# Taking turns between VectorE's SBUF copies and GpSimd's operations in a two-headed attention kernel

## The chip, the cores and the metric

The kernel runs on one core of a Trainium2 chip. A core has five engines with a queue of instructions each: TensorE (PE in the profile, its weight loads PEld), VectorE (DVE), ScalarE (ACT), GpSimd (POOL) and SyncE (SP, which only issues transfers here). Each engine works through its queue in order, and queues wait for each other by semaphores. The metric is the time of one execution on the device in microseconds, the median of several runs.

## The reference

Two attention blocks on inputs of 2048 tokens by 512 features, 32 heads of 16 features; their outputs stand side by side.

```python
def _A_ref(x, wqkv, wo):            # linear attention
    q, k, v = ...                   # x @ wqkv, split into 32 heads of 16
    phi = lambda t: jnp.where(t > 0, t + 1, jnp.exp(t)) + 1e-6
    pq, pk = phi(q), phi(k)
    kv = jnp.einsum("bhsd,bhse->bhde", pk, v)
    z = jnp.einsum("bhsd->bhd", pk)
    num = jnp.einsum("bhqd,bhde->bhqe", pq, kv)
    den = jnp.einsum("bhqd,bhd->bhq", pq, z)[..., None] + 1e-6
    return merge_heads(num / den) @ wo

def _B_ref(x, wqkv, wo):            # softmax attention, all 2048 keys
    q, k, v = ...
    p = _softmax(jnp.einsum("bhqd,bhkd->bhqk", q, k) * Dh ** -0.5)
    return merge_heads(jnp.einsum("bhqk,bhkd->bhqd", p, v)) @ wo

return jnp.concatenate([a, b], axis=-1)
```

## The kernel before

**The softmax block (B)** is nearly all of the work. The 32 heads are taken in four groups of eight (`Gp`). A unit is one group, one stretch of 512 queries (`c`) and the even or odd heads (`e_`), so there are 32 units. A unit has 64 blocks: 16 key tiles for each of four heads. A block is a score matmul (keys `KM` against queries `QT`, 128 keys by 512 queries), an exponential, and value matmuls (`VV`) that add into the PSUM bank `pPV` with the sum of the weights in a 17th column. Blocks go one of two ways:

- *ACT's way.* PE puts three or two blocks into the PSUM tile `pS0` or `pS1`, and one ACT instruction (L894) writes their exponentials to `PT`. One value matmul follows per block.
- *The way of VectorE and GpSimd.* PE puts a block into one of the two banks of `pD`. VectorE evicts it with a multiply and an add into 16-bit integers whose bits, read as floats, are a coarse exponential (`DI`, L806, "eviction" below). When two blocks are there, GpSimd adds two integer constants (`SHC`) to both in one operation of 128x1024 integers (L830, "shift" below), which gives two further copies of the coarse exponential at other phases. Three value matmuls follow per block, each with its own scaled copy of `VV`.

The two scaled copies of `VV` are made by VectorE from the first one (L573: 128x544 bf16, SBUF to SBUF, two for each of 16 groups of tiles). When a unit is finished, VectorE transposes `pPV` into `OT` (L989) and takes reciprocals (L994), and GpSimd multiplies (L995).

**The linear block (A)** is spread over the whole time as small jobs that use the same banks of `pD`. Where it needs phi, ACT takes an exponential into `EA` (L584), VectorE clamps it in place (L585: 128x256 or 128x512 bf16, SBUF to SBUF), and VectorE adds the positive part from PSUM (L587), which sets the bank free or is followed by the copy `VNa` (L599) that does. B's projections of later groups and the output projections (L673) are jobs of the same kind, and so is a small test of the inputs' size (`GR`, `FLG`). The keys' projection is spread over `KM` by 96 small transfers on SP's queue.

"Copies" below are the 32 instructions of L573 and the 48 of L585.

**What sets the order.** When the program is built, a planner lists for each engine what is ready, with an assumed duration, and picks the earliest start; between starts within 0.03 us the smaller priority goes first. What it picks goes into that engine's queue, and `Sched.add` derives the semaphore waits from what each operation reads and writes. An operation that reads a key waits for the last that wrote it, and one that writes it waits for all that read it. A key needs no memory behind it. The planner's constants:

- `DNEXT`: with fewer blocks left in a unit, VectorE's blocks are taken from the next unit. `ALAG`: no VectorE block is taken when a job of A or B is later than this (us).
- `P1`, `SH`: assumed durations of an eviction and a shift, for one or two blocks.
- `DEFER`, `FLOW`: a score round for ACT has priority 0 when its deadline is nearer than `DEFER` us (or all wanted banks of `pD` are free), and else `FLOW`. `DPR` is the priority of a score block for VectorE alone; jobs on PE have 2 to 2.5; rounds of value matmuls have 4, or 1 when `PVURG` or more blocks wait for theirs.

Between starts PE's gaps are filled with matmuls that only keep it busy (L1123, L1132).

Of the kernel before, what the change touches and what calls it, by code (L numbers as in the profile page):

```python
# [231 lines left out]
def bass_concat_heads__linear_attn_block__softmax_full_mha__prompt_kernel(nc, A_x, A_wqkv, A_wo, B_x, B_wqkv, B_wo, out):  # L232
# [12 lines left out]
    SHIFTS = (343, 685)  # L245
    VSCALE = (203.0 / 256.0, 161.0 / 256.0)
    UB = NT * 4
    DNEXT = 8
    DEND = 20
    TEND = 720.0  # L250
    ALAG = 20.0
    DLEAD = 1.0
    DBL = 3.0
    TRACE = None
# [5 lines left out]
    sch = Sched()  # L260
    es = contextlib.ExitStack()
    with es:
# [15 lines left out]
        VV = sb("VV", [128, 2, 3, NT * VST], BF)  # L278
        PT = sb("PT", [128, NPT, 5 * 512], F16)
        DI = sb("DI", [128, NDG, 3, 1024], I16)  # L280
        ZW = sb("ZW", [128, 32], BF)
        SHC = sb("SHC", [128, 4], I16)
# [6 lines left out]
        EA = sb("EA", [128, 2, 512], BF)  # L289
        OT = sb("OT", [128, 2, 512], F32)  # L290
        XN = OT.bitcast(BF)[:, 1, :].rearrange("p (x n) -> p x n", n=512)
        ZR = sb("ZR", [128, 2, 16], F32)
# [29 lines left out]
        def f32v(bk, n=512):  # L322
            return bk[0][:, bk[2]:bk[2] + n]
# [52 lines left out]
        for e_ in range(2):  # L376
            sch.add("dve", lambda e, e_=e_: e.tensor_reduce(PAR[:, e_:e_ + 1], ZMk[:].rearrange("p (a e) -> p e a", e=2)[:, e_, :],
                                                           axis=AX.X, op=ALU.max),
                    reads=["ZMk"], writes=[("PAR", e_)])
# [14 lines left out]
        T = {"pe": 0.0, "act": 0.0, "dve": 0.0, "pool": 0.0}  # L394
        cands = {k_: [] for k_ in T}
        tok = {}
        seq = [0]

        def push(eng, ready, prio, dur, run):
            seq[0] += 1  # L400
            cands[eng].append((ready, prio, seq[0], dur, run))

        class Job:

# [10 lines left out]
            def stage_done(self, i, end, bk, bi):  # L415
                if i == self.rel and bi is not None:
                    jfree[bi] = end + LAT
                for st, tk in self.gives:
                    if st == i:
                        tok[tk] = end + LAT  # L420
                if i + 1 < len(self.stages):
                    eng, dur, fn = self.stages[i + 1]
                    lat = LAT if eng != self.stages[i][0] else 0.0
                    push(eng, end + lat, self.prio if eng == "pe" else (0 if i + 1 <= self.rel and self.bank else min(self.prio, 2)), dur,
                         lambda st_, en_, fn=fn: (fn(bk), self.stage_done(i + 1, en_, bk, bi)))

        def f_pe(fn, reads):
            return lambda bk: sch.add("pe", lambda e: fn(e, bk), reads=reads, writes=[bk[3]])
# [2 lines left out]
            return lambda bk: sch.add(lane, lambda e: fn(e, bk), reads=[bk[3]] + list(reads), writes=writes)  # L431

        def f_op(lane, fn, reads=(), writes=()):
            return lambda bk: sch.add(lane, fn, reads=reads, writes=writes)

        MM, TRB = 0.2155, 0.0555
        PH = 0.11
        QK = 0.22
        pmode = [None]
        P1, SH = (0.61, 1.12), (1.1, 1.92)  # L440
        SLK = 0.0
        FMARG = 0.06
        DEFER, FLOW, DPR, DDEL = 0.5, 2.05, 3, 0
        PVR, PVMIN, PVURG = 3, 4, 24
        jfree = [0.0] * 2 + [None] * 5

        def copy_to(lane, out_fn, in_fn):
# [110 lines left out]
        def v4_job(t4, Gp, **kw):  # L558
            r = Gp % 2

            def mm(e, bk, i):
                tl, cc = divmod(i, 4)
                t = 4 * t4 + tl
                return e.matmul(f32v(bk)[:, tl * 128:(tl + 1) * 128], lhsT=xTb[:, cc, t * 128:(t + 1) * 128],  # L564
                                rhs=Wb[:, cc, 1024 + Gp * 128:1024 + Gp * 128 + 128], start=(cc == 0), stop=(cc == 3))
            ts = range(4 * t4, 4 * t4 + 4)
            st = halves(mm, [("Wb", 2)] + [("xTb", t) for t in ts], n=16, parts=2, dur=0.0555)
            v = [VV[:, r, k_, 4 * t4 * VST:(4 * t4 + 4) * VST] for k_ in range(3)]
            st.append(("dve", 0.6, f_ev("dve", lambda e, bk: e.tensor_copy(  # L569
                v[0].rearrange("p (h c) -> p h c", c=17)[:, :, 0:16],  # L570
                f32v(bk).rearrange("p (h d) -> p h d", d=16)), [("VV1", r)], [("VV", r, 0, t4)])))
            for k_ in range(2):
                st.append(("dve", 0.21, f_op("dve", lambda e, k_=k_: e.tensor_scalar(v[k_ + 1], v[0], VSCALE[k_], None, op0=ALU.mult),  # L573
                                             [("VV", r, 0, t4), ("VV1", r)], [("VV", r, k_ + 1, t4)])))
            return Job(st, [("xTb", t) for t in ts] + ([("pvdone", Gp - 2)] if Gp >= 2 else []), [(4, ("V", Gp, t)) for t in ts], rel=2, **kw)


# [2 lines left out]
        def phi_stages(c0, n, out_ap, okeys):  # L580
            q = ectr[0] % 2
            ectr[0] += 1
            return [
                ("act", 0.051 + n * 0.000833, f_ev("act", lambda e, bk: e.activation(EA[:, q, 0:n], f32v(bk)[:, c0:c0 + n], ACTF.Exp), [], [("EA", q)])),  # L584
                ("dve", 0.067 + n * 0.00026, f_op("dve", lambda e: e.tensor_scalar(EA[:, q, 0:n], EA[:, q, 0:n], 1.0, 1e-6, op0=ALU.min, op1=ALU.add),  # L585
                                               [("EA", q)], [("EA", q)])),
                ("dve", 0.067 + n * 0.00105, f_ev("dve", lambda e, bk: e.scalar_tensor_tensor(out_ap, f32v(bk)[:, c0:c0 + n], 0.0, EA[:, q, 0:n],  # L587
                                                                                          op0=ALU.max, op1=ALU.add), [("EA", q)], okeys))]

# [170 lines left out]
        def d_pick(at, used):  # L760
# [5 lines left out]
            if (ajobs and at > ajobs[0].ready + ALAG) or (bjobs and at > bjobs[0].ready + ALAG and bjobs[0].start_time() is not None):  # L766
                return None
            if u < NU - 1 and left[u] < DNEXT:
                u += 1
# [52 lines left out]
        def shifts(buf):  # L822
            s_ = gst[buf]
            n = len(s_["items"])
            if not s_["closed"] or s_["p1"] < n:
                return

            def go(st_, en_):
                w = 256 * n
                sch.add("pool", lambda e: e.tensor_tensor(  # L830
                    DI32[:, buf, 1:3, 0:w], DI32[:, buf, 0, 0:w].unsqueeze(1).broadcast_to([128, 2, w]),
                    SHC32[:].unsqueeze(2).broadcast_to([128, 2, w]), op=ALU.add),
                    reads=[("DI", buf, 0, i) for i in range(n)] + ["SHC"], writes=[("DI", buf, k_, i) for k_ in (1, 2) for i in range(n)])
                for k_ in (1, 2):
                    for i in range(n):
                        done(buf, k_, i, en_)
            push("pool", s_["t"] + LAT, 1, SH[n - 1], go)
# [147 lines left out]
        def unit_done(u, t_):  # L985

            xb = (u // 2) % 2
            Gp, c, e_ = unit(u)
            sch.add("dve", lambda e: e.transpose(OT[:, 0, :], PVb[:, 0:512]), reads=[("PV", g) for g in range(4)], writes=[("OT", 0)])  # L989
            pvopen[0] = t_ + LAT  # L990
            o = OT[:, 0, :].rearrange("p (b r) -> p b r", r=32)
            xn = XN[:, xb, :].rearrange("p (b r) -> p b r", r=32)
            zr = ZR[:, 0, 0:16]
            st = [("dve", 0.25, f_op("dve", lambda e: e.reciprocal(zr, o[:, :, 16]), [("OT", 0)], [("ZR", 0)])),  # L994
                  ("pool", 0.65, f_op("pool", lambda e: e.tensor_tensor(xn[:, :, 16 * e_:16 * e_ + 16], o[:, :, 0:16],  # L995
                                                                      zr.unsqueeze(2).broadcast_to([128, 16, 16]), op=ALU.mult),
                                    [("OT", 0), ("ZR", 0)], [("XN", xb, e_)]))]
            if e_ == 1:
                k = 4 * Gp + c
                st.append(("dve", 0.65, f_op("dve", lambda e: e.transpose(ON[:, k, :], XN[:, xb, :]), [("XN", xb, 0), ("XN", xb, 1)], on_keys(k))))  # L1000
            urgent.append(Job(st, [("ot", u - 1)] if u else [], [(1, ("ot", u))] + ([(2, ("on", Gp, c))] if e_ == 1 else []),
                              bank=False, ready=t_ + LAT, prio=0.5))
            if Gp == NGP - 1 and e_ == 1:
                fin = u == NU - 1
                for tl in range(4):
                    ln = ("dve", "act")[tl % 2] if fin else "dve"
                    urgent2.append(omm_job("b", 4 * c + tl, 1 + tl, [("on", Gp, c)], [(1, ("st", c, tl))], lane=ln))
# [135 lines left out]
        while True:  # L1143
            opts = []
            for eng in T:
                best = None
                for c_ in cands[eng]:
                    st = max(T[eng], c_[0])
                    k_ = (round(st / 0.05), c_[1], c_[2])
                    if best is None or k_ < best[0]:  # L1150
                        best = (k_, st, c_)
                if best is not None:
                    c_ = best[2]
                    opts.append(pe_opt(best[1], c_[1], c_[3], c_[4], c_, "f") if eng == "pe" else (best[1], c_[1], eng, c_[3], c_[4], c_))
# [28 lines left out]
            st, _, eng, dur, run_, c_ = o  # L1183
            if c_ is not None:
                cands[eng].remove(c_)
            if eng == "pe":
                filler(st - T["pe"])
            T[eng] = st + dur
            run_(st, st + dur)
            npick += 1  # L1190
            if TRACE is not None:
# [88 lines left out]
```

## Time and profile before

| | |
|---|---|
| time, median of 3 runs | 759.22 us (758.39 to 762.62) |
| profiled execution: its own time | 765.03 us |
| profiled execution: span from first to last instruction | 763.3 us |
| mean granted PE clock in it | 0.97 |
| instructions profiled | 15604 |

All rows of the profile come from that one execution. "Busy" is the time in which an engine's instructions run, and an instruction that is held after its start counts as busy. "Idle before" of a group is the time for which its engine stood still just before its instructions, with the engine and line that ended it. PE's instructions overlap each other, so PE's busy share is no measure of how full it is.

### The profile page before, as it was taken

How to read it: one execution, taken by the hardware profiler on the slowest of the kernel's cores; microseconds unless marked ns; L12 is line 12 of the kernel's file. 1: busy time of each engine (PE TensorE's matmuls, PEld its weight loads, DVE VectorE, ACT ScalarE, POOL GpSimd, SP SyncE). 2: the span in 40 equal slices, each digit the busy share in tenths (PEclk: the TensorE clock that was granted, in tenths of full speed). 3: DMA queues.
4: the chain of work that ended last, by engine and by line, in shares of the span. 5: the costliest groups of instructions: out<-in, count | busy, mean ns of one | idle time of the engine just before them, and what ended most of it. 6: DMA issues, size and time to landing. Idle time of an engine off the chain costs nothing.

```text
span 763.3 us, 15604 instructions
## 1 busy us (share of the span) xinstructions
PE 695.0 (91%) x6655; PEld 231.4 (30%) x6706; DVE 569.6 (75%) x930; ACT 697.2 (91%) x646; POOL 561.4 (74%) x339
## 2 busy tenths in 40 slices
PE   8999798999999998998999898999899989899987
PEld 4334433233333333321222222322222212222222
DVE  5788787777777787776888787787778777778661
ACT  6899689899999898987999989989899979999993
POOL 4596357577889677565899968796679957879990
PEclk9999999999999999998999999999999989999999
DMA  9800000000000000100100000000010000011001
GB/s 207 207 2 1 2 1 9 8 8 9 1 2 1 2 1 2 36 8 8 22 16 21 9 1 15 22 17 20 8 28 15 22 1 29 16 42 28 19 12 31
DMA packets 35788, 17.33 MB, mean 23 GB/s; under 512 B 26496, under 2 KB 35200, under 8 KB 35712
## 3 DMA queue, kind: packets, MB, share of 16 engines
q1 hardware_dynamic: 34912, 15.87, 8.4%
q8 instruction: 54, 0.88, 0.5%
q10 hardware_dynamic: 800, 0.39, 0.2%
q14 instruction: 22, 0.18, 0.1%
HBM read 4.72 MB, written 4.19 MB: 12 GB/s over the span
## 4 chain that ended last, share of the span: by engine, by line
ACT 57%; PE 28%; DVE 14%; issue 1%; POOL 0%; POOLq 0%
ACT PT L894 55%; PE pPV L969 9%; PE pS L725 6%; DVE DI L806 5%; DVE EA L585 3%; PE pD L725 3%; PE pD L480 2%; PE pD L595 2%; PE pD L564 2%; DVE VV L573 2%; ACT EA L584 1%; PE pD L673 1%; PE pD L620 1%; DVE VV L569 1%; DVE KNa L587 1%
## 5 line engine op out<-in xcount | busy, mean ns | idle before, releaser
L894 ACT ACTIVATE PT<-pS 128x1536 f16<-128x1536 f32 (+1 forms) x591 | 682.9, 1323 | 41.7 <-PE pD L725 25.6
L830 POOL TENSOR_TENSOR DI<-DI,SHC 128x1024 int32<-128x1024 int32 x286 | 535.7, 1894 | 173.3 <-DVE DI L806 169.4
L806 DVE TENSOR_SCALAR DI<-pD 128x512 int16<-128x512 f32 (+1 forms) x551 | 375.6, 704 | 117.5 <-PE pD L725 107.0
L969 PE MATMUL pPV<-DI,VV 128*17 128x512 f16 x1716 | 275.5, 390 | 1.0 <-DVE OT L989 1.0
L969 PE MATMUL pPV<-PT,VV 128*17 128x512 f16 x1476 | 266.8, 389 | 0.3
L725 PE MATMUL pS<-QT,KM 32*128 32x512 bf16 x1476 | 232.9, 391 | 19.5 <-ACT PT L894 14.1
L725 PE MATMUL pD<-QT,KM 32*128 32x512 bf16 x572 | 206.1, 393 | 18.9 <-DVE DI L806 8.6
L725 PEld LDWEIGHTS pS<-QT,KM 32*128 32x128 bf16 x1476 | 55.8, 91 | 218.2 <-ACT PT L894 159.8
L969 PEld LDWEIGHTS pPV<-DI,VV 128*17 128x17 bf16 x1716 | 57.5, 88 | 77.4 <-issue 57.7
L969 PEld LDWEIGHTS pPV<-PT,VV 128*17 128x17 bf16 x1476 | 56.6, 88 | 60.5 <-issue 48.1
L725 PEld LDWEIGHTS pD<-QT,KM 32*128 32x128 bf16 x572 | 49.0, 91 | 76.9 <-DVE DI L806 44.2
L585 DVE TENSOR_SCALAR EA<-EA 128x256 bf16<-128x256 bf16 (+1 forms) x48 | 35.1, 732 | 10.1 <-ACT EA L584 9.7
L595 PE MATMUL pD<-Wa,xTa 128*128 128x128 bf16 x512 | 38.4, 225 | 3.0 <-DVE DI L806 2.6
L480 PE MATMUL pD<-xTb,Wb 128*128 128x512 bf16 x100 | 30.6, 400 | 5.7 <-DVE DI L806 2.4
L989 DVE STREAM_TRANSPOSE OT<-pPV 128x512 f32<-128x512 f32 x32 | 22.7, 710 | 16.6 <-PE pPV L969 16.6
L595 PEld LDWEIGHTS pD<-Wa,xTa 128*128 128x128 bf16 x512 | 30.2, 101 | 15.7 <-DVE DI L806 9.2
L995 POOL TENSOR_TENSOR OT<-OT,ZR 128x256 bf16<-128x256 f32 x32 | 20.0, 625 | 16.0 <-DVE ZR L994 16.0
L584 ACT ACTIVATE EA<-pD 128x256 bf16<-128x256 f32 (+1 forms) x48 | 24.7, 515 | 5.4 <-PE pD L595 4.8
L564 PE MATMUL pD<-Wb,xTb 128*128 128x128 bf16 x256 | 19.6, 228 | 3.0 <-DVE DI L806 2.3
L573 DVE TENSOR_SCALAR VV<-VV 128x544 bf16<-128x544 bf16 x32 | 19.9, 649 | 0.2
L620 PE MATMUL pD<-xTa,Wa 128*128 128x512 bf16 x57 | 17.2, 407 | 3.1 <-DVE PQT L587 1.8
L564 PEld LDWEIGHTS pD<-Wb,xTb 128*128 128x128 bf16 x256 | 15.5, 102 | 10.0 <-DVE DI L806 5.1
(89 smaller groups left out, 272.4 us busy)
## 6 DMA issues: line engine op xcount, KB each, us to landing
out_dram<-OB SPq DMA_DIRECT2D x16, 128.0 KB, 1.7
out_dram<-KNa SPq DMA_DIRECT2D x16, 128.0 KB, 1.7
Wa<-in_A_wqkv_dram SPq DMA_DIRECT2D x1, 1536.0 KB, 8.1
KM<-KR SPq DMA_DIRECT2D x96, 16.0 KB, 1.8
Wb<-in_B_wqkv_dram SPq DMA_DIRECT2D x2, 384.0 KB, 6.0
Wb<-in_B_wqkv_dram SPq DMA_DIRECT2D x1, 512.0 KB, 4.3
WOa<-in_A_wo_dram SPq DMA_DIRECT2D x1, 512.0 KB, 8.8
VNa<-in_B_wo_dram SPq DMA_DIRECT2D x1, 512.0 KB, 3.4
```

Of the source, the lines that this page charges most:

```text
L480: return e.matmul(f32v(bk), lhsT=Wb[:, cc, kind * 512 + Gp * 128:kind * 512 + Gp * 128 + 128], rhs=xTb[:, cc, sc * 512:(sc + 1) * 512], st ...
L564: return e.matmul(f32v(bk)[:, tl * 128:(tl + 1) * 128], lhsT=xTb[:, cc, t * 128:(t + 1) * 128], rhs=Wb[:, cc, 1024 + Gp * 128:1024 + Gp * ...
L573: st.append(("dve", 0.21, f_op("dve", lambda e, k_=k_: e.tensor_scalar(v[k_ + 1], v[0], VSCALE[k_], None, op0=ALU.mult), [("VV", r, 0, t4) ...
L584: ("act", 0.051 + n * 0.000833, f_ev("act", lambda e, bk: e.activation(EA[:, q, 0:n], f32v(bk)[:, c0:c0 + n], ACTF.Exp), [], [("EA", q)])),
L585: ("dve", 0.067 + n * 0.00026, f_op("dve", lambda e: e.tensor_scalar(EA[:, q, 0:n], EA[:, q, 0:n], 1.0, 1e-6, op0=ALU.min, op1=ALU.add), [ ...
L595: return e.matmul(f32v(bk)[:, 128 * x:128 * x + 128], lhsT=xTa[:, cc, (t + i_) * 128:(t + i_ + 1) * 128], rhs=Wa[:, cc, c0:c0 + 128], star ...
L620: return e.matmul(f32v(bk), lhsT=Wa[:, cc, bq * 128:(bq + 1) * 128], rhs=xTa[:, cc, sc * 512:(sc + 1) * 512], start=(cc == 0), stop=(cc == 3))
L725: return e.matmul(dst, lhsT=KM[32 * g:32 * g + 32, Gp % 2, e_, j * 128:(j + 1) * 128], rhs=QT[32 * g:32 * g + 32, Gp % 2, c * 512:(c + 1) ...
L806: sch.add("dve", lambda e: e.tensor_scalar(DI[:, buf, 0, i * 512:(i + n) * 512], DB[:, bi * 512:(bi + n) * 512], ESC, EB, op0=ALU.mult, op ...
L830: sch.add("pool", lambda e: e.tensor_tensor(DI32[:, buf, 1:3, 0:w], DI32[:, buf, 0, 0:w].unsqueeze(1).broadcast_to([128, 2, w]), SHC32[:]. ...
L894: sch.add("act", lambda e: e.activation(PT[:, row, c0:c0 + w], SCR[sl][:, 0:w], ACTF.Exp, scale=SC), reads=skeys(sl), writes=[("PT", row, ...
L969: sch.add("pe", lambda e, g=g, vk=vk, c0=c0, P=P, first=first, last_=last_: e.matmul(PVb[32 * g:32 * g + 17, 0:512], lhsT=VV[:, Gp % 2, vk ...
```

## The change

VectorE's 80 copies get a written key, `PORT`, and GpSimd's shifts and its multiplication of finished units read that key. So a copy waits by semaphore until all earlier shifts and multiplications in the planner's order have ended, and the next one of GpSimd waits until the copy has ended. In the planner a copy is marked with `lock`: it may start only when GpSimd's planned work has ended, and GpSimd's next planned start is moved behind it. Eight constants are changed too.

```diff
-    DNEXT = 8
+    DNEXT = 16
...
-    ALAG = 20.0
+    ALAG = 10.0
...
-        def push(eng, ready, prio, dur, run):
+        def push(eng, ready, prio, dur, run, lock=False):
             seq[0] += 1
-            cands[eng].append((ready, prio, seq[0], dur, run))
+            cands[eng].append((ready, prio, seq[0], dur, run, lock))
...
                     push(eng, end + lat, self.prio if eng == "pe" else (0 if i + 1 <= self.rel and self.bank else min(self.prio, 2)), dur,
-                         lambda st_, en_, fn=fn: (fn(bk), self.stage_done(i + 1, en_, bk, bi)))
+                         lambda st_, en_, fn=fn: (fn(bk), self.stage_done(i + 1, en_, bk, bi)), "PORT" in getattr(fn, "keys", ()))
...
         def f_op(lane, fn, reads=(), writes=()):
-            return lambda bk: sch.add(lane, fn, reads=reads, writes=writes)
+            op = lambda bk: sch.add(lane, fn, reads=reads, writes=writes)
+            op.keys = writes
+            return op
...
-        P1, SH = (0.61, 1.12), (1.1, 1.92)
+        P1, SH = (0.61, 1.12), (1.05, 1.86)
...
-        DEFER, FLOW, DPR, DDEL = 0.5, 2.05, 3, 0
-        PVR, PVMIN, PVURG = 3, 4, 24
+        DEFER, FLOW, DPR, DDEL = 0.15, 3.5, 4.2, 0
+        PVR, PVMIN, PVURG = 3, 4, 32
...
-                                             [("VV", r, 0, t4), ("VV1", r)], [("VV", r, k_ + 1, t4)])))
+                                             [("VV", r, 0, t4), ("VV1", r)], [("VV", r, k_ + 1, t4), "PORT"])))
...
-                                               [("EA", q)], [("EA", q)])),
+                                               [("EA", q)], [("EA", q), "PORT"])),
...
-                    reads=[("DI", buf, 0, i) for i in range(n)] + ["SHC"], writes=[("DI", buf, k_, i) for k_ in (1, 2) for i in range(n)])
+                    reads=[("DI", buf, 0, i) for i in range(n)] + ["SHC", "PORT"], writes=[("DI", buf, k_, i) for k_ in (1, 2) for i in range(n)])
...
-                                    [("OT", 0), ("ZR", 0)], [("XN", xb, e_)]))]
+                                    [("OT", 0), ("ZR", 0), "PORT"], [("XN", xb, e_)]))]
...
-                    st = max(T[eng], c_[0])
+                    st = max(T[eng], c_[0], T["pool"] if c_[5] else 0.0)
...
             T[eng] = st + dur
+            if c_ is not None and c_[5]:
+                T["pool"] = max(T["pool"], st + dur)
```

The planner makes another order from this on all engines. Lines of the changed kernel are two to four higher (an eviction is L808, a copy of `VV` L575, one of `EA` L587, a shift L832). Counted over the whole order, ACT gets 602 exponentials of scores instead of 591 (by shape 301 of 128x1536 for 295, 300 of 128x1024 for 295 and one of 128x512 in both); score blocks in `pD` are 544 for 572; evictions are 534 of one block for 530 and 5 of two for 21; shifts are 272 for 286.

VectorE's queue before, at the second group of `VV` tiles of the second head group. `s_pool`, `s_act`, `s_pe` and `s_dve` are the engines' semaphores that a row waits for.

```order
L585 TENSOR_SCALAR EA<-EA 128x256 [waits s_act]
L587 SCALAR_TENSOR_TENSOR KNa<-pD,EA 128x256 [waits s_dve]
L599 CAST VNa<-pD 128x2x128
L569 CAST VV<-pD 128x32x16 [waits s_pe]
L806 TENSOR_SCALAR DI<-pD 128x512 [waits s_pe]
L573 TENSOR_SCALAR VV<-VV 128x544 [waits s_dve]
L573 TENSOR_SCALAR VV<-VV 128x544
L806 TENSOR_SCALAR DI<-pD 128x512 [waits s_pe]
L527 TENSOR_TENSOR OA<-pD,identf 128x512 [waits s_pe]
```

The same queue now, at the same group:

```order
L571 CAST VV<-pD 128x32x16 [waits s_pe]
L808 TENSOR_SCALAR DI<-pD 128x512 [waits s_pe]
L575 TENSOR_SCALAR VV<-VV 128x544 [waits s_pool,s_dve]
L808 TENSOR_SCALAR DI<-pD 128x512 [waits s_pe]
L529 TENSOR_TENSOR OA<-pD,identf 128x512 [waits s_pe]
L808 TENSOR_SCALAR DI<-pD 128x512 [waits s_pe]
L575 TENSOR_SCALAR VV<-VV 128x544 [waits s_pool]
L808 TENSOR_SCALAR DI<-pD 128x512 [waits s_pe]
L533 TENSOR_REDUCE GRX<-OA 128x1
L808 TENSOR_SCALAR DI<-pD 128x512 [waits s_pe]
L587 TENSOR_SCALAR EA<-EA 128x256 [waits s_pool,s_act]
```

The two copies of a pair no longer stand side by side, evictions and a masking (L529) have moved between them, and copies now wait for GpSimd. Over the whole order 64 of the 80 copies have a wait for `s_pool`.

PE's queue before, late in the program, where the output projection of B (`VNa` holds its weights by then) stands among score rounds:

```order
L725 MATMUL pS<-QT,KM 128x512 x2
L725 MATMUL pD<-QT,KM 128x512
L725 MATMUL pS<-QT,KM 128x512 x3
L673 MATMUL pD<-VNa,ON 128x512 x2
L969 MATMUL pPV<-DI,VV 17x512
L969 MATMUL pPV<-PT,VV 17x512
```

and now:

```order
L727 MATMUL pS<-QT,KM 128x512 x3
L675 MATMUL pD<-VNa,ON 128x512 x4
L727 MATMUL pS<-QT,KM 128x512 x2
L675 MATMUL pD<-VNa,ON 128x512 x2
L727 MATMUL pS<-QT,KM 128x512 x3
L727 MATMUL pD<-QT,KM 128x512
L971 MATMUL pPV<-DI,VV 17x512 x3
```

Projection matmuls have moved ahead of ACT's score rounds (into `pS`) and part them from each other. PE changes between score, value and other matmuls 1306 times in its whole row of work, before 1253 times.

## The prediction

> **What bounds the kernel now.** I read the page's busy table first, then busy time by stretch, the groups by shape, one stall in order of time, and the waits.
>
> ```profile
> span 763.3 us, 15604 instructions
> PE 695.0 (91%) x6655; PEld 231.4 (30%) x6706; DVE 569.6 (75%) x930; ACT 697.2 (91%) x646; POOL 561.4 (74%) x339
> 0.00:12.00 12.00, 9.02 (x72) 6.24 (x73) 4.93 (x12) 4.82 (x7) 7.23 (x21) 1.00 0.90 208
> 12.00:40.00 28.00, 26.89 (x242) 9.42 (x241) 20.73 (x36) 25.01 (x22) 15.11 (x9) 0.94 0.83 193
> 40.00:740.00 700.00, 642.30 (x6251) 210.54 (x6298) 540.85 (x879) 656.52 (x609) 534.37 (x307) 0.97 0.05 13
> 740.00:763.30 23.30, 16.79 (x94) 5.21 (x95) 3.07 (x5) 10.84 (x12) 4.71 (x4) 0.96 0.08 26
> ```
>
> In a stretch's row the columns are its length, then PE, PEld, DVE, ACT and POOL busy (instructions), the granted clock, and DMA. ACT is busy 697.2 of 763.3 us. Its busy time is nearly pure exponentials of at most 1.5 us each. Of its 66.1 us idle, the first 40 us hold 10.2 and the last 23.3 hold 12.5; the middle 700 us hold 43.5. So the time is ACT's work, plus two ends that the change leaves alone, plus those 43.5 us. PE's 91% is pipelined busy time, and PE waits for ACT far more than ACT for PE:
>
> ```profile
> PEld pS L725 <- ACT PT L894: 159.8, 348, 0.9
> ACT PT L894 <- PE pD L725: 25.6, 31, 2.1
> PEld pPV L969 <- issue: 105.8, 417, 0.8
> PEld pPV L969 <- POOL DI L830: 1.9, 8, 0.3
> ```
>
> (us in total, times, longest.) The groups by shape carry the prices (us in all, mean ns of one):
>
> ```profile
> L830 POOL TENSOR_TENSOR DI<-DI,SHC 128x1024 int32<-128x1024 int32 x286 | 535.7, 1894 | 173.3 <-DVE DI L806 169.4 <-DVE GR L550 2.8
> L894 ACT ACTIVATE PT<-pS 128x1536 f16<-128x1536 f32 x295 | 452.7, 1535 | 36.4 <-PE pD L725 21.5 <-PE pS L725 14.0
> L806 DVE TENSOR_SCALAR DI<-pD 128x512 int16<-128x512 f32 x530 | 350.1, 684 | 107.3 <-PE pD L725 97.2 <-PE pS L725 5.4
> L894 ACT ACTIVATE PT<-pS 128x1024 f16<-128x1024 f32 x295 | 328.4, 1113 | 5.3 <-PE pD L725 4.1 <-PE pS L725 0.9
> L806 DVE TENSOR_SCALAR DI<-pD 128x1024 int16<-128x1024 f32 x21 | 25.5, 1215 | 10.2 <-PE pD L725 9.8 <-PE pS L725 0.4
> L585 DVE TENSOR_SCALAR EA<-EA 128x256 bf16<-128x256 bf16 x32 | 20.1, 627 | 8.1 <-ACT EA L584 8.0
> L573 DVE TENSOR_SCALAR VV<-VV 128x544 bf16<-128x544 bf16 x32 | 19.9, 649 | 0.2
> L585 DVE TENSOR_SCALAR EA<-EA 128x512 bf16<-128x512 bf16 x16 | 15.1, 942 | 2.0 <-ACT EA L584 1.7
> L585 DVE TENSOR_SCALAR EA<-EA x48: 215/400/2012, 68.5 to 647.5; 128x256 bf16<-128x256 bf16 x32, 128x512 bf16<-128x512 bf16 x16
> L551 DVE SCALAR_TENSOR_TENSOR GR<-GR 1x1 f32<-1x1 f32 x1 | 1.9, 1893 | 0.0
> ```
>
> The EA copies take 215 ns at best and 2012 at worst (minimum, median and maximum in their second row); at 0.25 us each the 80 copies would need 20 us of VectorE, and they hold it for 55.1. One single-element operation with two SBUF operands takes 1893 ns, the time of one shift. What a slow copy does stands in order of time (start, length, in brackets the idle time before):
>
> ```profile
> 246.33 1.89 POOL L830 TENSOR_TENSOR DI<-DI,SHC 128x1024 int32<-128x1024 int32 x1 [0.37 <-DVE DI L806]
> 246.69 1.61 DVE L585 TENSOR_SCALAR EA<-EA 128x256 bf16<-128x256 bf16 x1 [0.44 <-ACT EA L584]
> 249.41 1.89 PE L564 MATMUL pD<-Wb,xTb 128*128 128x128 bf16 x16 [1.07 <-DVE DI L806]
> 251.89 1.45 ACT L894 ACTIVATE PT<-pS 128x1536 f16<-128x1536 f32 x1 [2.06 <-PE pD L725]
> 246.70:249.30 2.60, 1.16 (x12) 0.29 (x8) 2.56 (x4) 2.60 (x3) 1.52 (x1) 1.00 0.00 0
> 249.34:252.76 3.42, 3.35 (x29) 1.99 (x29) 1.77 (x6) 1.36 (x2) 0.06 (x1) 0.50 0.02 5
> ```
>
> The copy starts inside a shift and ends 0.08 us after it (248.30 against 248.22): it was held for about 1.4 us. The evictions behind it in VectorE's queue come late, PE idles 1.07 us for a bank, the clock falls to 0.50 for 3.4 us, and ACT starves for 2.06 us.
>
> The size of that: I took the 22 copies longer than 1 us and cut out, from each one's start to 5 us after its end, 18 merged stretches; and the rest of 40 to 740 us beside them. First, last and sum of each:
>
> ```profile
> 54.20:60.60 6.40, 5.45 (x58) 2.15 (x58) 5.47 (x10) 6.10 (x6) 3.85 (x3) 1.00 0.02 4
> 625.40:632.10 6.70, 5.33 (x50) 1.40 (x47) 6.07 (x9) 6.11 (x6) 3.96 (x3) 1.00 0.06 19
> sum 141.50, PE 114.89 PEld 39.55 DVE 115.74 ACT 112.56 POOL 80.60; mean PE 6.38 PEld 2.20 DVE 6.43 ACT 6.25 POOL 4.48
> 40.00:54.20 14.20, 13.58 (x158) 5.14 (x161) 11.45 (x17) 14.20 (x14) 13.99 (x9) 1.00 0.00 1
> 632.10:740.00 107.90, 100.88 (x938) 28.16 (x946) 81.25 (x124) 106.83 (x97) 89.99 (x52) 1.00 0.09 25
> sum 558.50, PE 527.41 PEld 170.99 DVE 425.11 ACT 543.96 POOL 453.78; mean PE 27.76 PEld 9.00 DVE 22.37 ACT 28.63 POOL 23.88
> ```
>
> Behind slow copies ACT idles 28.9 of 141.5 us, elsewhere 14.5 of 558.5 (2.6%). At 2.6% those stretches would idle 3.6, so up to **25.3 us** hang on slow copies.
>
> **The change part by part.** (a) *More work for ACT.* Counted from the order, the new plan gives VectorE and GpSimd 544 score blocks instead of 572 and ACT 28 more: 6 exponentials of 1535 ns and 5 of 1113 ns, 9.2 + 5.6 = **+14.8 us**. ACT is the bound, nothing hides this, and all of it counts.
>
> (b) *Less for the others.* 14 shifts of 1894 ns fewer, 26.5 us of POOL. Evictions: 16 fewer of 1215 ns and 4 more of 684 ns, 16.7 us off VectorE. PE has 56 value matmuls fewer and 26 keep-warm ones more. None of these engines ends the middle stage, so I cost it at nothing; it only makes (c) likelier. If ACT ceased to be the bound, it would count.
>
> (c) *The turns.* In the new order 64 of the 80 copies wait for GpSimd's semaphore, 45 EA and 19 VV. The plan puts a copy where it believes the running shift has ended, with evictions ahead of it (the second VV pair of the second head group is now parted by two evictions and a masking, before by nothing). Behind a waiting copy stand KNa's or PQT's second half, VNa and the next evictions, and PE waits for their banks. The gain lies between nothing (the wait only changes its name) and 25.3 us. I take the upper end: that is the row of the stretches with no slow copy, and (b) leaves GpSimd more gaps.
>
> (d) *The handover.* Its price is the step from VectorE to GpSimd at the kernel's end:
>
> ```profile
> 751.09 0.25 DVE L994 RECIPROCAL ZR<-OT 128x16 f32<-128x16 f32 x1
> 751.42 0.62 POOL L995 TENSOR_TENSOR OT<-OT,ZR 128x256 bf16<-128x256 f32 x1 [7.33 <-DVE ZR L994]
> ```
>
> 0.08 us. For the 45 EA copies, which hold a bank meanwhile, **+3.6 us**; the bounds are 0 (beside ACT's work) and 5.1 (64). In the other direction a shift now waits for the last copy, and behind it POOL's whole queue, the normalising of a finished unit included. PE waits 1.9 us for shifts now and POOL idles 173 us for its input, so some 0.3 us per copy there is covered; if that cover goes, PE's value matmuls are late next.
>
> (e) *The new constants.* A score round for ACT may now be put off until 0.15 us before its deadline instead of 0.5, behind projection work. PE's row of work changes kind 1306 times instead of 1253, counted from the order. I cost that at nothing, since PE has waits for ACT to spend (159.8 us above); its price without that cover is the second rival. SP issues the same 96 spreading transfers, some in other places; none is waited for long enough to enter. The start and the last 12 keep-warm matmuls before the final projection stay.
>
> Sum on the profiled execution: 763.3 + 14.8 - 25.3 + 3.6 = 756.4 us of span. That execution took 765.03 us, 1.7 beyond its span and 0.77% above the median of 759.22. So (756.4 + 1.7) x 759.22 / 765.03 = **752.4 us**, 0.9% faster. I call 0.5% (3.8 us) what a measurement can tell from no change. To break even 18.4 of the 25.3 us must go, to be faster by 0.5% some 22.
>
> **The rivals**, each carried to the median in the same way.
>
> *The wait takes the stall's place (slower).* VectorE stands idle before the copy where it was held inside it; ACT's idle time stays: 763.3 + 14.8 + 3.6 = 781.7, 777.5 us. For it: the copy still cannot run beside a shift. Against it: the order around copies is changed. Half the stalls staying gives 764.9. The Trainium skill, page "SBUF — State Buffer", section "Who interferes with whom", says that GpSimd and a two-port VectorE operation exclude each other for a whole instruction, whoever starts first; the trace agrees (0.08 us behind the shift). By that rule alone a semaphore starts no copy earlier, and the sum would be this rival's 777.5; only the order can gain.
>
> *PE refills ACT late (slower).* The row "pPV L969 <- issue" has 105.8 us in 417 times, 0.25 us per change of work; 53 more, if all fall on ACT, are 13.4 us: 765.6. It decides from 7 us on, some 12 ns per refill over 602. Against it: PE's waiting for ACT.
>
> *The clock drops stay.* Ten stretches between 92 and 622 us at 0.50, first, last and sum:
>
> ```profile
> 92.33:95.74 3.41, 3.41 (x36) 3.13 (x37) 2.03 (x5) 0.47 (x2) 0.00 (x0) 0.50 0.02 5
> 614.57:621.40 6.83, 6.39 (x33) 1.20 (x35) 4.18 (x8) 3.40 (x4) 4.53 (x3) 0.50 0.01 2
> sum 40.96, PE 39.39 PEld 11.71 DVE 22.47 ACT 23.36 POOL 23.37; mean PE 3.94 PEld 1.17 DVE 2.25 ACT 2.34 POOL 2.34
> ```
>
> ACT idles 17.6 us in them. If other idle time of PE sets them off, only 25.3 - 17.6 = 7.7 us go: 769.9. Against it: a slow copy ends shortly before each. The Trainium skill, page "TensorE: Matmul & The Clock Gate", section "HAM oscillation — how this bites in real kernels", asks for a PE idle gap above about 3.4 us; by that rule gaps of 1.07 us would not cause the drops, and this rival would hold. The trace differs: the clock fell after 2.6 us with PE busy 1.16.
>
> *More goes.* Half of the other 14.5 us vanishes as well, VectorE and GpSimd being lighter: 749.1 of span, 745.2.
>
> **How the numbers follow.** Forecast 0.47 (of that 0.06 within 0.5%); more goes 0.12; part of the stalls stays 0.15 (0.08 within, 0.07 slower); late refills 0.12 (0.05 within, 0.07 slower); clock drops stay 0.07; the wait takes the place 0.07. Faster 0.41 + 0.12 = 0.53, same 0.19, slower 0.28. The likeliest case alone spans 747 to 757. The range, 742 to 771, leaves out the full waiting rival and the far ends.
>
> **What would show it.** Right: EA and VV copies all near 0.2 to 0.3 us, ACT busy about 712 us with about 18 us idle in the middle, few stretches at 0.50. (c) is wrong if VectorE's idle time before L575 and L587 by GpSimd nears the 35 us by which the copies were too long; (d) if PE waits for shifts; (e) if ACT's waits for pS grow while copies are short. The prediction fails if ACT's middle idle time stays above 25 us.

## The result, and the profile after

| | before | changed |
|---|---|---|
| median | 760.92 us (758.39 to 764.22, 4 runs) | 737.27 us (734.46 to 740.72, 4 runs) |
| ratio, 95% interval | | 0.969 [0.963, 0.975] |
| span of the profiled execution | 763.3 us | 738.8 us |

The change makes the kernel 3.1% faster. Its time is 15 us below the forecast of 752.4 us and below the range, which began at 742. The page's first lines, then busy time by stretch (columns as in the prediction: length, PE, PEld, DVE, ACT, POOL, clock, DMA); the last stretch has the length of the last one before:

```profile
span 738.8 us, 15635 instructions
PE 694.7 (94%) x6677; PEld 229.5 (31%) x6677; DVE 519.3 (70%) x918; ACT 704.7 (95%) x657; POOL 535.0 (72%) x325
0.00:40.00 40.00, 35.35 (x313) 15.27 (x317) 28.02 (x52) 30.78 (x30) 22.03 (x29) 1.00 0.84 198
40.00:715.50 675.50, 642.82 (x6286) 209.64 (x6280) 488.25 (x862) 664.66 (x619) 510.32 (x295) 0.99 0.05 13
715.50:738.80 23.30, 16.49 (x85) 4.62 (x80) 3.07 (x5) 9.26 (x10) 2.63 (x3) 0.91 0.09 26
```

ACT's idle time in the middle fell from 43.5 us to 10.8 (675.50 less 664.66). The whole difference, from ACT's side: 7.5 us more work, 32.6 less idle in the middle, 1.0 less at the start, 1.6 more at the end; 763.3 + 7.5 - 32.6 - 1.0 + 1.6 = 738.8.

The copies by line (minimum, median and maximum in ns), the groups that were shown of before, and the waits:

```profile
L587 DVE TENSOR_SCALAR EA<-EA x48: 186/227/296, 62.5 to 614.5; 128x256 bf16<-128x256 bf16 x32, 128x512 bf16<-128x512 bf16 x16
L575 DVE TENSOR_SCALAR VV<-VV x32: 291/301/304, 12.9 to 482.8; 128x544 bf16<-128x544 bf16 x32
L832 POOL TENSOR_TENSOR DI<-DI,SHC 128x1024 int32<-128x1024 int32 x272 | 509.7, 1891 | 174.2 <-DVE DI L808 148.0 <-DVE EA L587 15.6 <-DVE VV L575 9.4
L896 ACT ACTIVATE PT<-pS 128x1536 f16<-128x1536 f32 x602 | 692.4, 1336 | 14.4 <-PE pD L727 11.1
DVE EA L587 <- POOL DI L832: 8.4, 13, 2.1
ACT PT L896 <- PE pS L727: 3.0, 7, 0.6
```

No copy is held any more (the longest took 2012 ns of EA and 2004 of VV before, now 296 and 304). The wait has gone to the other side: GpSimd's shifts stand back 25.0 us for copies (15.6 + 9.4), while VectorE waits for shifts 8.4 us ahead of EA copies and 1.7 us ahead of VV copies. Half clock in the middle fell from ten stretches, 41.0 us, to three; first, last and sum:

```profile
134.02:137.43 3.41, 3.31 (x26) 0.63 (x26) 2.06 (x5) 2.98 (x3) 3.41 (x3) 0.50 0.00 0
591.40:598.23 6.83, 6.83 (x39) 1.11 (x38) 4.34 (x8) 5.76 (x7) 6.06 (x4) 0.50 0.01 2
sum 13.65, PE 13.55 PEld 2.64 DVE 7.17 ACT 11.04 POOL 11.50; mean PE 4.52 PEld 0.88 DVE 2.39 ACT 3.68 POOL 3.83
```

### The profile page after: what moved, and what is told of

It reads as the page before. It is cut to its first block, busy times and chain, and to the rows that moved or that the text cites. A ratio compares the mean times of both kernels' runs of the same rounds, so it can differ in the third digit from the quotient of the medians.

```text
span 738.8 us, 15635 instructions
## 1 busy us (share of the span) xinstructions
PE 694.7 (94%) x6677; PEld 229.5 (31%) x6677; DVE 519.3 (70%) x918; ACT 704.7 (95%) x657; POOL 535.0 (72%) x325
## 4 chain that ended last, share of the span: by engine, by line
ACT 77%; PE 17%; DVE 2%; POOL 1%; DMA 1%; SPq 1%; issue 1%; DVEq 0%
ACT PT L896 75%; PE pPV L971 6%; PE pS L727 4%; ACT EA L586 2%; POOL DI L832 1%; PE pD L675 1%; PE pD L482 1%; DVE DI L808 1%; PE pD L566 1%; PE pD L597 1%; DMA xTb<-in_B_x_dram 1%; PE pD L727 1%; PE pD L1134 1%; SPq L344 1%; PE pD L622 0%
## 5 line engine op out<-in xcount | busy, mean ns | idle before, releaser
L896 ACT ACTIVATE PT<-pS 128x1536 f16<-128x1536 f32 x602 | 692.4, 1336 | 14.4 <-PE pD L727 11.1
L832 POOL TENSOR_TENSOR DI<-DI,SHC 128x1024 int32<-128x1024 int32 x272 | 509.7, 1891 | 174.2 <-DVE DI L808 148.0
L808 DVE TENSOR_SCALAR DI<-pD 128x512 int16<-128x512 f32 x539 | 359.8, 689 | 122.1 <-PE pD L727 114.2
L971 PE MATMUL pPV<-PT,VV 128*17 128x512 f16 x1504 | 251.0, 386 | 1.1 <-ACT PT L896 0.8
L971 PE MATMUL pPV<-DI,VV 128*17 128x512 f16 x1632 | 243.5, 387 | 2.2 <-DVE OT L991 1.8
L727 PE MATMUL pD<-QT,KM 32*128 32x512 bf16 x544 | 194.6, 387 | 5.8 <-DVE DI L808 3.5
L971 PEld LDWEIGHTS pPV<-DI,VV 128*17 128x17 bf16 x1632 | 52.5, 88 | 75.3 <-issue 55.3
L991 DVE STREAM_TRANSPOSE OT<-pPV 128x512 f32<-128x512 f32 x32 | 22.8, 711 | 15.2 <-PE pPV L971 14.8
L587 DVE TENSOR_SCALAR EA<-EA 128x256 bf16<-128x256 bf16 (+1 forms) x48 | 11.8, 245 | 18.5 <-POOL DI L832 8.4
L675 PE MATMUL pD<-WOa,ONT 128*128 128x512 bf16 x64 | 18.5, 383 | 0.1
L571 DVE CAST VV<-pD 128x512 bf16<-128x512 f32 x16 | 11.0, 689 | 8.2 <-PE pD L566 8.2
```

What stands on the lines that cost most here:

```text
L675: return e.matmul(f32v(bk), lhsT=src, rhs=WO[:, hb, :], start=(hb == 0), stop=(hb == 3))
L727: return e.matmul(dst, lhsT=KM[32 * g:32 * g + 32, Gp % 2, e_, j * 128:(j + 1) * 128], rhs=QT[32 * g:32 * g + 32, Gp % 2, c * 512:(c + 1) ...
L808: sch.add("dve", lambda e: e.tensor_scalar(DI[:, buf, 0, i * 512:(i + n) * 512], DB[:, bi * 512:(bi + n) * 512], ESC, EB, op0=ALU.mult, op ...
L832: sch.add("pool", lambda e: e.tensor_tensor(DI32[:, buf, 1:3, 0:w], DI32[:, buf, 0, 0:w].unsqueeze(1).broadcast_to([128, 2, w]), SHC32[:]. ...
L896: sch.add("act", lambda e: e.activation(PT[:, row, c0:c0 + w], SCR[sl][:, 0:w], ACTF.Exp, scale=SC), reads=skeys(sl), writes=[("PT", row, ...
L971: sch.add("pe", lambda e, g=g, vk=vk, c0=c0, P=P, first=first, last_=last_: e.matmul(PVb[32 * g:32 * g + 17, 0:512], lhsT=VV[:, Gp % 2, vk ...
```

## The experiments

The change has three parts: the lock in the planner (another order), the waits (the key `PORT`), and the constants. Theory A: the planned order makes the gain. Theory B: the constants. Theory C: the waits.

**One part at a time.** Waits alone, on the order of before:

```diff
-   ... [("VV", r, k_ + 1, t4)]   ... [("EA", q)]   ... + ["SHC"]   ... [("OT", 0), ("ZR", 0)]
+   ... [("VV", r, k_ + 1, t4), "PORT"]   ... [("EA", q), "PORT"]   ... + ["SHC", "PORT"]   ... [("OT", 0), ("ZR", 0), "PORT"]
```

> The order and constants of before, with only the shared key added: 58 of the 80 copies now wait by semaphore for GpSimd. If the order makes the gain (theory A) or the constants do (theory B), this is within 1% of before (about 761 us): VectorE stands idle before the copies for the 35 us by which they were too long before, ACT keeps 40 us or more idle in the middle, and some ten stretches stay at half clock. If the waits themselves make it (theory C), the time falls by 10 us or more.

757.2 us against 760.5, ratio 0.997 [0.994, 0.999]. The waits of that run by total:

```profile
DVE EA L585 <- POOL DI L830: 27.5, 20, 2.2
DVE VV L573 <- POOL DI L830: 11.9, 8, 2.0
POOL DI L830 <- DVE EA L585: 14.4, 18, 2.1
ACT PT L894 <- PE pS L725: 14.5, 20, 2.2
```

VectorE now stands idle ahead of the copies for some 40 us where it was held inside them for 36 (their time beyond 0.25 us each). ACT still idles 37.2 us in the middle, and seven stretches, 23.9 us, stay at half clock. Both are somewhat less than A and B expected, but in the main the wait only renames the stall on that order. C as the whole cause is out.

The changed kernel with the constants of before (lock and waits):

```diff
-    DNEXT = 16; ALAG = 10.0; SH = (1.05, 1.86); DEFER, FLOW, DPR = 0.15, 3.5, 4.2; PVURG = 32
+    DNEXT = 8;  ALAG = 20.0; SH = (1.1, 1.92);  DEFER, FLOW, DPR = 0.5, 2.05, 3;   PVURG = 24
```

> The changed kernel with the eight constants of before: lock in the planner and waits, 564 score blocks for VectorE. Theory A (the planned turns remove the stalls): at least two thirds of the gain, 745 us or less, ACT idle in the middle under 25 us, few stretches at half clock. Theory B (the constants): 755 us or more, and stalls before copies that stay.

736.6 us, ratio 0.969 [0.963, 0.974]: the whole gain, with no stretch at half clock in the middle, where ACT idles 15.4 us (671.70 less 656.25):

```profile
40.00:711.70 671.70, 641.81 (x6294) 211.50 (x6294) 501.62 (x875) 656.25 (x613) 528.47 (x304) 1.00 0.05 13
```

The constants alone (the reverse of that diff on before):

> Before with the eight new constants, no lock and no waits: 562 score blocks for VectorE, copies planned as if they were alone. Theory A: copies are still held for 30 us or so in all, and the time is above 750 us. Theory B: 743 us or less although copies are held.

770.8 us, ratio 1.012 [1.006, 1.018]: slower by 1.2%, clear of the noise. Copies are still held (mean 612 ns of VV and 614 of EA, before 649 and 732), and ACT idles 47.0 us in the middle:

```profile
L585 DVE TENSOR_SCALAR EA<-EA 128x256 bf16<-128x256 bf16 (+1 forms) x48 | 29.5, 614 | 18.8 <-ACT EA L584 18.5
L573 DVE TENSOR_SCALAR VV<-VV 128x544 bf16<-128x544 bf16 x32 | 18.6, 612 | 0.3
40.00:751.00 711.00, 663.42 (x6338) 215.96 (x6337) 524.25 (x876) 664.00 (x613) 527.90 (x305) 0.97 0.05 12
```

Theory B is out; A stands so far.

**The same orders without the waits.** Keys for the planner alone, in the changed kernel:

```diff
-    op = lambda bk: sch.add(lane, fn, reads=reads, writes=writes)
+    op = lambda bk: sch.add(lane, fn, reads=reads, writes=[w for w in writes if w != "PORT"])
     # and no "PORT" among the reads of GpSimd's two operations
```

> The changed kernel's order word for word, without the semaphore waits between copies and GpSimd. Theory A: the time of the changed kernel (737 us) within 1%, since the order already keeps the two apart; copies are held for under 10 us in all. Theory C: the copies are held for 20 us or more, and the time is 745 us or more.

737.6 us, ratio 0.971 [0.965, 0.977], as with the waits: A again. But the same edit with the constants of before:

> The lock in the planner with the eight constants of before, and no semaphore waits between copies and GpSimd. Theory A (the planned order is the whole gain): 733 to 738 us, as the same order with waits (736.6), copies held for 5 to 15 us in all. Rival (the waits protect the order from drift): 742 us or more, copies held for over 20 us.

753.3 us (745 to 756 over 12 runs), ratio 0.991 [0.988, 0.994], where the waits on that order gave 736.6. Here A in its plain form fell: the order is not enough. One place in both runs shows why. Without the waits (first the EA copies by minimum, median and maximum, then start, length, idle before):

```profile
L587 DVE TENSOR_SCALAR EA<-EA x48: 216/227/1992, 68.0 to 609.4; 128x256 bf16<-128x256 bf16 x32, 128x512 bf16<-128x512 bf16 x16
333.96 1.89 POOL L832 TENSOR_TENSOR DI<-DI,SHC 128x1024 int32<-128x1024 int32 x1 [0.46 <-DVE DI L808]
334.01 1.99 DVE L587 TENSOR_SCALAR EA<-EA 128x512 bf16<-128x512 bf16 x1
337.25 1.45 ACT L896 ACTIVATE PT<-pS 128x1536 f16<-128x1536 f32 x1 [1.02 <-PE pS L727]
```

and with them:

```profile
330.83 0.29 DVE L587 TENSOR_SCALAR EA<-EA 128x512 bf16<-128x512 bf16 x1
331.20 1.89 POOL L832 TENSOR_TENSOR DI<-DI,SHC 128x1024 int32<-128x1024 int32 x1 [0.88 <-DVE EA L587]
```

The plan has the copy first. Without a wait the shift, ready 0.05 us sooner, goes out of turn, the copy is held for 1.7 us and ACT idles 1.02 us. With it GpSimd waits 0.88 us, and there nobody waits for GpSimd. Of the 14 copies held for over 0.5 us in the run without waits, 9 were held by a shift that the plan puts behind them. So lock and waits work together: the lock gives an order in which copies fall into GpSimd's gaps, and the wait makes GpSimd keep it. With the new constants there are 10 shifts fewer (272 for 282), copies were held for 9.9 us against 19.6 (beyond 0.25 us each, as above), and the waits had little left to do.

The fourth corner of the table, waits on the order of the constants alone:

> The new constants and the waits, no lock in the planner: the order of the kernel with the constants alone (770.8 us), copies now waiting for GpSimd. If waits on an order that was planned without the port only rename the stall: 765 to 771 us. If they help because a shift stands back for the copy whenever the two come out of turn: 760 us or less.

771.9 us, ratio 1.017 [1.013, 1.022]: as without the waits, so there too they rename. This run also bears on the clock. Its middle, and the three stretches at half clock in it, summed:

```profile
40.00:746.70 706.70, 651.61 (x6330) 214.35 (x6329) 497.51 (x876) 660.61 (x612) 525.83 (x304) 0.99 0.05 12
sum 13.65, PE 13.50 PEld 4.60 DVE 8.27 ACT 6.43 POOL 8.87; mean PE 4.50 PEld 1.53 DVE 2.76 ACT 2.14 POOL 2.96
```

The half clock lasts as long as in the changed kernel (13.65 us), and ACT idles 46.1 us all the same, where it idles 10.8 there. So the clock drops alone do not make the loss.

| median us (ratio) | neither | waits alone | lock alone | lock and waits |
|---|---|---|---|---|
| old constants | 760.5 (1) | 757.2 (0.997) | 753.3 (0.991) | 736.6 (0.969) |
| new constants | 770.8 (1.012) | 771.9 (1.017) | 737.6 (0.971) | 737.3 (0.969) |

Each ratio is to the kernel before in the same set of runs (760.5 to 760.9, 759.6 or 759.0 us). Each corner is one order out of the planner; other orders of the same kind were not tried.

**Who can pay for a turn.** Theory D: GpSimd has slack and VectorE has none. To the kernel with lock, waits and old constants (736.6 us) I added work that nobody reads, on one engine and on the other:

```diff
+    JNK = ...     # on GpSimd, ahead of every ninth shift
+    e.memset(JNK[:], 1.0)
```


> Turns and waits with the constants of before, and 31 writes of about 1.2 us more on GpSimd, ahead of every ninth shift, 38 us in all, written to a place that nobody reads. Theory D (GpSimd has slack and VectorE has none, so that a turn should be paid by GpSimd): under 743 us against 736.6. Rival (a late shift costs ACT as much as a late eviction): 755 us or more.

```diff
+    JNK = ...     # on VectorE, ahead of every second EA copy
+    e.tensor_reduce(JNK[...], xTb[:, 0, 0:1400], axis=AX.X, op=ALU.max)
```


> The same kernel, with 24 operations of about 1.5 us more on VectorE ahead of every second EA copy, 36 us in all (a maximum that nobody reads). Theory D: 760 us or more, ACT idle in the middle 35 us or more, half-clock stretches back. Rival: the waits soak it up: under 750 us.

The first row is of the GpSimd run, the second of the VectorE run (times in ns), then the middle of each:

```profile
L835 POOL MEMSET JNK<- x31: 1161/1164/1167, 30.8 to 704.2; 128x1280 bf16 x31
L588 DVE TENSOR_REDUCE JNK<-xTb x24: 1599/1610/1612, 67.9 to 638.9; 128x1 f32<-128x1400 bf16 x24
40.00:719.00 679.00, 645.12 (x6288) 212.93 (x6288) 501.68 (x875) 657.33 (x612) 561.10 (x335) 1.00 0.05 13
40.00:759.90 719.90, 662.40 (x6292) 215.47 (x6292) 536.89 (x899) 661.41 (x611) 527.54 (x304) 0.97 0.05 12
```

On GpSimd 36.1 us (31 x 1.164) made it 744.6, 8.0 us more, just over the 743 that I gave D. On VectorE 38.6 us (24 x 1.61) made it 783.9, 47 us more: ACT's middle idle time went from 15.4 to 58.5 us, and twelve stretches fell to half clock, though no copy was held (the longest took 303 ns). GpSimd's shifts stood back 50.6 us for copies in that run and 29.3 us without the additions, so part of the 47 us may have come by way of GpSimd. The same operation in the order without waits:

> The order of the run above with one VectorE operation more ahead of every second EA copy, 24 in all: a maximum over 1400 elements that nobody reads, about 1.5 us each, 36 us, as long as the copies were held in the kernel before, but clear of GpSimd and unknown to the planner. Theory A1 (VectorE's lateness is what cost ACT its time, by whatever cause): 753 us or more, ACT idle in the middle 30 us or more, half-clock stretches come back. Rival A2 (what cost time was GpSimd and VectorE keeping each other from their memory port): under 745 us, VectorE's slack takes it.

790.3 us against that order's 753.3: 37 us for 38.4 us put in, while copies were held for 11.8 us instead of 19.6. It is VectorE's lateness ahead of EA copies that costs ACT its time, about a microsecond for each, and a held copy is one way to be late. The pieces on the two engines differ in size and place, so the two prices show an order of size and no exact ratio.

**Which copies.** Turns for EA alone (`PORT` taken from the writes of the VV copies):

> Turns with the old constants, but for the 48 EA copies alone; the 32 copies of VV are planned as free again. If a held copy costs the same wherever it stands, the VV copies, which were held for 11 of the 36 us, give back about a third of the gain: 744 us. If only copies that hold a bank of pD matter (EA), the time stays at 737 us within 0.5%.

738.4 us, ratio 0.973 [0.969, 0.976], within 0.5% of the turns for all. The VV copies were held again:

```profile
L575 DVE TENSOR_SCALAR VV<-VV x32: 283/294/2004, 13.7 to 474.2; 128x544 bf16<-128x544 bf16 x32
L575 DVE TENSOR_SCALAR VV<-VV 128x544 bf16<-128x544 bf16 x32 | 16.6, 540 | 0.3
```

That is 9.3 us beyond 0.25 us each (32 x 0.29), and the median rose by 1.8 us. The intervals overlap, so whether the 32 VV copies matter at all stays open; a third of the gain they do not hold.

**A faster version.** The 12 keep-warm matmuls ahead of the last projection are planned at a price of 0.22 us (the first at 0.33) and take 0.45 each. Given that price there are 6:

```diff
-                    cost = MM + (PH if pmode[0] != "f" else 0.0)    # filler on a bank of pD
+                    cost = 0.45
```

> The first kernel of this list with a true price (0.45 us instead of 0.22 or 0.33) for the keep-warm matmuls into pD: 6 instead of 12 stand before the last projection, nothing else moves. In the changed kernel they end at 730.3 us, some 2 to 3 us after the last unit's transpose. If PE's row alone sets the end: 2 to 2.7 us less than the first kernel. Rival: the clock falls to half and the last 16 matmuls of 0.22 us take 0.43, which gives 1.7 to 3.5 us back: no change.

On the unsteady order without waits it gave 751.4 (743 to 753) against 753.3, ratios 0.987 [0.983, 0.991] and 0.991 [0.988, 0.994]: unclear. On the order with waits and old constants:

> Turns and waits with the constants of before (736.6 us), and 6 instead of 12 keep-warm matmuls ahead of the last projection; all else in the same order. If PE's row alone sets the end: 2 to 2.7 us less, 734 us, the fastest version here. Rival: the clock falls to half in the tail and gives it back: 736 to 738 us.

733.4 us (733.0 to 735.0, 5 runs), ratio 0.965 [0.962, 0.967], the fastest here: 3.2 us under the same kernel with 12 (736.3 to 736.8), where I expected 2 to 2.7. The intervals of the two ratios overlap. PE's tail with 12 and with 6:

```profile
721.20 5.34 PE L1134 MATMUL pD<-identb 128*128 128x512 bf16 x12
726.60 1.90 PE L675 MATMUL pD<-VNa,ON 128*128 128x512 bf16 x8
722.56 2.64 PE L1134 MATMUL pD<-identb 128*128 128x512 bf16 x6
725.26 1.90 PE L675 MATMUL pD<-VNa,ON 128*128 128x512 bf16 x8
```

The projection follows 2.70 us after their start instead of 5.40, and its matmuls take no longer.

## Why the prediction was right or wrong

The mechanism was right, held copies make VectorE late and ACT starves. Three terms of the sum were mis-sized, all to the same side: the span came out 17.6 us shorter than the 756.4 of the sum, of which (a) is 7.3, (c) 7.3 and (d) 3.6, less 0.6 at the two ends.

**(c), the turns: 25.3 us forecast, 32.6 measured.** With lock, waits and the old constants ACT still idles 15.4 us in the middle, 2.3%, near the 2.6% that the prediction took as a background that stays; so the turns took away 28.0 of the 43.5 us. The other 4.6 us went with the new constants (10.8 us of 675.5, 1.6%). The failed step is that (e) put the constants at nothing on ACT's idle time, and to a smaller part, 2.7 us, the cut at 5 us behind copies longer than 1 us. How the constants do it was not tested, and each of these figures is from one profiled execution.

A simpler price would have come close, read from these runs afterwards and not tested by itself: EA copies were held for 23 us before (35.1 less 48 x 0.25), a delay ahead of EA copies cost about itself, and held VV copies little. The turns gained 24 us with the old constants (760.5 to 736.6).

**(a), ACT's extra work: 14.8 us forecast, 7.5 measured.** The step that failed is the mean length of one exponential taken as its cost. Neighbours overlap in the trace. Before, 19 in a row, and the first three of them alone, were

```profile
728.66 20.99 ACT L894 ACTIVATE PT<-pS 128x1536 f16<-128x1536 f32 x19
728.66 1.45 ACT L894 ACTIVATE PT<-pS 128x1536 f16<-128x1536 f32 x1
730.00 1.02 ACT L894 ACTIVATE PT<-pS 128x1024 f16<-128x1024 f32 x1
730.91 1.46 ACT L894 ACTIVATE PT<-pS 128x1536 f16<-128x1536 f32 x1
```

One of 1536 columns is followed after 1.34 us and one of 1024 after 0.91, where their mean lengths are 1.535 and 1.113. Six and five more at those distances are 12.6 us. The group's busy time grew by 9.5 us, from

```profile
L894 ACT ACTIVATE PT<-pS 128x1536 f16<-128x1536 f32 (+1 forms) x591 | 682.9, 1323 | 41.7 <-PE pD L725 25.6
```

to 692.4, my reading being that with fewer gaps more of them overlap; what took the other 2.0 us off ACT's total was not followed up. The constants are what costs: with lock, waits and the old constants ACT's work was 695.9 us, 1.3 less than before, with 594 exponentials for 591, and the new constants added eight more and 8.8 us. The page "ScalarE: Activation LUTs" of the Trainium skill, section "What ACT_TABLE_LOAD costs", says that activations back to back overlap by about 93 ns; the start of this row agrees with 0.11 us (1.45 less 1.34), and against the mean length it is 0.20.

**(d), the handover: 3.6 us forecast, nothing seen** that could be told from (c); the two together were forecast to take 21.7 us of idle time away, and 32.6 went. The handover fell on GpSimd, which stood back 25.0 us for copies and had the room. The price of 0.08 us was not tested by itself.

**(b)** held: no other engine took over (PE got 27 keep-warm matmuls more, 67 for 40, and not 26). **(e)** held for the waits it named: ACT's waits for `pS` fell from 14.9 us to 4.4 with the turns and to 3.0 with the new constants, though PE changes work more often.

The rivals: *the wait takes the stall's place* is what the waits do on an order planned without the port (757.2 us, 771.9). The Trainium skill, page "SBUF — State Buffer", section "Who interferes with whom", agrees there; what its rule does not give is the 17 us between 753.3 and 736.6, which come from who goes first. *The clock drops stay* was wrong: they went with the stalls (41.0 us to 13.7, none with the old constants) and came back, twelve stretches, with 1.61 us operations on VectorE. PE's longest gap in that middle was 1.8 us, as before the change; that is half of the 3.4 us that the Trainium skill, page "TensorE: Matmul & The Clock Gate", section "HAM oscillation — how this bites in real kernels", asks for, so the trace does not agree with that rule. *Late refills* did not come: "pPV <- issue" has 101.4 us in 423 times, before 105.8 in 417. *More goes* (745.2) was the nearest, with a chance of 0.12; with (a) at its measured 7.5 it would have given 738. It named the 7.3 us of idle time that went beyond the 25.3; that VectorE's and GpSimd's lighter load took them, as it says, is not shown.

## What to carry to other kernels

Where operations of two engines hold each other up, find which engine has slack and let that one wait: plan the other's short copies into its gaps, and add the semaphore so that it keeps the order. With the old constants the waits alone gave 0.3%, the planned order alone 0.9%, both 3.1%; with the new ones the order alone gave 2.9%. Price a stall by putting one of the same size back, on either engine and at the place in question, and price an added instruction by the distance between starts, not by its mean duration. New constants that come with a change need their own run: here they were worth nothing beside lock and waits, 16 us beside the lock alone, and cost over 1% without either.

## What the hardware showed

A copy that a shift holds counts as busy, so the wait shows in no list of waits, only as a maximum of 2012 ns beside a minimum of 215. And 36 to 39 us of delay in pieces of 1.2 to 1.6 us cost 8 us on GpSimd but 37 to 47 us on VectorE. In the middle of each of the two VectorE runs PE fell to half clock twelve times; how much of the 47 us is the clock and how much the wait itself was not separated. The clock also fell where PE hardly paused: before the three drops left in the changed kernel's middle, no gap of PE there was longer than 0.6 us, and the cause of those drops stays open.
